# Sliding-window attention followed by a wave MLP: a reworked start, earlier and later loads, and a new order around the stage changes

## The chip, the cores and the metric

The kernel runs on one core of a Trainium2 chip. The metric is device time in microseconds (us) of one execution. Executions of one kernel on one chip mostly lie within 1 us of each other, and an effect of half a per cent is 0.9 us, so every claim below about time rests on a ratio of means with its 95% interval, and profiles (each is one execution) are used for where the time goes. An execution more than 1.5% above the fastest of its kernel is called slow and left out of the ratios.

## The reference

Four batches, eight heads, 768 positions, head size 64. Attention keeps the last 96 positions and 8 global ones, with a bias that falls linearly with distance. Its output x goes through a "wave" layer:

```
theta = x @ w_theta                       # 512 x 512
u     = x + w_tok_r @ (x*cos(theta)) + w_tok_i @ (x*sin(theta))    # tokens mixed, 768 x 768
out   = u + relu(u @ w_ch)                # 512 x 512
```

## The kernel before

The program first runs the attention of batch 0 in an order written by hand, then weaves the wave layer of batch b (dense work for TensorE) with the attention of batch b+1. Five engines take part: PE (TensorE), DVE (VectorE), ACT (ScalarE), POOL (GpSimd, which issues all loads that turn f32 into bf16, on one software queue, q0) and SP (SyncE, which issues output writes and the DMA transposes of x, u and of q and k of batch 3). An engine executes its instructions in program order. Where one instruction waits, all behind it on that engine wait too.

Loads of batch 3 come in "token" form, 128 tokens on the partitions, so that a DMA transpose can turn q and k without reordering copies. Each row is 64 numbers of f32, 256 bytes:

```python
def load_qk_tokens(b, h0, n):
    qk = loads[b][0]
    for h in range(h0, h0 + n):
        for i_ in range(2):
            pair = qk[:, i_, h // 2 * 2:h // 2 * 2 + 2].rearrange("p h t d -> p (h t d)")
            nc.gpsimd.dma_start(
                out=pair.rearrange("p (t h d) -> p t h d", t=NT, h=2)[:, :, h % 2],
                in_=(q, k)[i_][b, h].rearrange("(t p) d -> p t d", p=T))
```

Half of q and k of batch 3 is loaded while batch 0 is in its wave layer, the rest and v behind a gate, a GpSimd copy of one element of the transposed x of batch 1:

```python
def load_behind(b, tile):
    g = nc.gpsimd.tensor_copy(out=gate, in_=tile).ins
    with tc.issue_after(g):
        load_qk_tokens(b, H // 2, H // 2)
        load_all_v(b)
```

`kglob` builds kG from kT: k of each block with the 8 global positions copied over its front. In batch 3 these copies stand on VectorE among the products `zri` = x*cos, x*sin:

```python
def kglob(b, p):
    kT = qkT[(b, p)][1]
    kG = qkT[(b, p)][2] = att.tile([T, NT - 2, T], BF, name="kG", bufs=6)
    with behind("dve") if b == B - 1 else nullcontext():
        nc.vector.tensor_copy(out=kG, in_=kT[:, T:(NT - 1) * T].rearrange(...))
        nc.vector.tensor_copy(out=kG[:, :, 0:NG], in_=kT[:, None, 0:NG].to_broadcast(...))
```

The start of a batch: `th` are the six parts of theta, `rest` what is left of the channel step of the batch before.

```python
order = th[:4] + rest[:2] + th[4:] + rest[2:] if b else []
if b == 2:
    order[:0] = [lambda p=p: prep_dma(3, p) for p in range(1, NP)]   # DMA transposes of q, k
if b == 1:
    order.insert(0, lambda: load_behind(3, xT_sb[1][0:1, NC - 1, 0:1]))
```

The loop over head pairs in the attention of batch 0, cut. Each turn ends with the scores of the next pair and the transposes of the one after it:

```python
for p in range(NP):
    score_exp(0, p, 1)
    ...                                  # out0: kT on ACT, qT on DVE; kglob
    values(0, p - 1, 0); values(0, p - 1, 1)
    score_bias(p, 2); score_mms(0, p, 2); score_exp(0, p, 2)
    cast0(p + 2, 1, dve); cast0(p + 2, 0, dve)       # reordering copies
    ...
    score_bias(p + 1, 0); score_mms(0, p + 1, 0); score_exp(0, p + 1, 0)
    score_bias(p + 1, 1); score_mms(0, p + 1, 1)
    turn0(p + 2, 1); turn0(p + 2, 0)                 # 12 transposes
    ...
```

The softmax here doesn't subtract the row's maximum and nothing guards it: scores larger than these inputs give would overflow.

## Time and profile before

| | before |
|---|---|
| median of 3 executions | 175.34 us (175.04 to 175.66) |
| span of the profiled execution | 172.6 us |
| PE / DVE / ACT / POOL busy | 93 / 74 / 57 / 22% |
| first cosine of batches 0, 1, 2, 3 starts at | 29.91, 74.19, 108.03, 141.99 us |
| last u of batch 1 to first u of batch 2 | 105.60 to 117.72: 12.1 us |

The cosines are good milestones: each opens the wave layer of a batch, since ScalarE can start one only when x of that batch is complete, transposed and multiplied by `w_theta`. The lines of the profile that show what bounds the kernel are in the prediction below.

### The profile page before, as it was taken

To read this page: it belongs to the slowest core of one execution; us is meant where nothing else is said; L and a number is where in the kernel's file an instruction comes from. 1 tells how busy PE (TensorE), PEld (TensorE's weight loads), DVE (VectorE), ACT (ScalarE), POOL (GpSimd) and SP (SyncE) were. 2 spreads that over 40 slices of the span, in tenths; PEclk is the share of its full clock that TensorE was granted. 3 is DMA by queue.
4 is the path that set the end of the run, shared out by engine and by line. 5 is a ranking of instruction groups with operands and counts; after the bars stand their busy time and mean duration, and the time that the engine had idled before them with its cause. 6 is when DMAs were issued, how large, how long until landed. Compare 5 with 4: busy or idle time off the path is not lost.

```text
span 172.6 us, 3652 instructions
## 1 busy us (share of the span) xinstructions
PE 159.9 (93%) x1482; PEld 83.5 (48%) x1482; DVE 128.5 (74%) x288; ACT 99.1 (57%) x124; POOL 37.9 (22%) x45
## 2 busy tenths in 40 slices
PE   6479979999999999999999998999999989999991
PEld 1245655455756566544455463444554634444440
DVE  7678965678999999999587588597786837724443
ACT  2479676999497595489834740979348308500010
POOL 8974355005272010099300000000000000000000
PEclk9999999999999999999999999999999999999998
DMA  5999999999999999879999997787138571323335
GB/s 146 192 193 178 210 208 209 204 204 171 160 204 175 166 155 128 132 97 154 210 141 80 224 158 165 138 152 226 30 76 113 135 171 40 142 41 102 100 93 182
DMA packets 75088, 25.92 MB, mean 150 GB/s; under 512 B 63168, under 2 KB 72128, under 8 KB 75072
## 3 DMA queue, kind: packets, MB, share of 16 engines
q0 software_dynamic: 45680, 12.45, 78.4%
q1 hardware_dynamic: 28976, 12.72, 36.6%
q10 hardware_dynamic: 416, 0.52, 0.9%
q8 instruction: 11, 0.18, 0.4%
q14 instruction: 5, 0.04, 0.1%
HBM read 25.69 MB, written 6.29 MB: 185 GB/s over the span
## 4 chain that ended last, share of the span: by engine, by line
PE 59%; DVE 21%; ACT 10%; DMA 6%; issue 1%; SPq 0%; DVEq 0%; ACTq 0%
PE ps L409 29%; PE ps L434 10%; PE pb L389 5%; PE pb L295 4%; PE pb L352 4%; DVE x_sb L362 4%; ACT etab L142 3%; PE ps L389 3%; ACT e L302 3%; DMA qk<-in_k_dram 3%; DVE kG L218 2%; DVE e L312 2%; ACT cs L395 2%; DMA kT<-qk 2%; DMA xT<-x_sb 2%; PE ps L244 2%
## 5 line engine op out<-in xcount | busy, mean ns | idle before, releaser
L409 PE MATMUL ps<-zri,w_tokT 128*128 128x512 bf16 x288 | 70.6, 380 | 0.3 <-DVE o_sb L440 0.2
L302 ACT ACTIVATE e<-pb 128x1024 bf16<-128x1024 f32 (+1 forms) x48 | 43.6, 958 | 23.1 <-PE pb L295 22.9
L409 PEld LDWEIGHTS <-w_tokT 128*128 128x128 bf16 x288 | 26.1, 98 | 29.0 <-issue 1.0
L414 DVE TENSOR_TENSOR u<-x_sb,ps 128x512 bf16<-128x512 bf16 x24 | 16.4, 682 | 14.6 <-PE ps L409 14.6
L434 PE MATMUL ps<-w_ch_bf,uT 128*128 128x512 bf16 x96 | 24.2, 379 | 0.0
L398 DVE TENSOR_TENSOR zri<-x_sb,cs 128x512 bf16<-128x512 bf16 x48 | 17.9, 418 | 8.0 <-ACT cs L395 7.8
L440 DVE SCALAR_TENSOR_TENSOR o_sb<-ps,u 128x512 f32<-128x512 f32 (+1 forms) x25 | 16.5, 662 | 3.1 <-PE ps L434 3.1
L395 ACT ACTIVATE cs<-pb,halfpi 128x1024 bf16<-128x1024 f32 x8 | 8.9, 1116 | 15.7 <-PE pb L389 15.7
L312 DVE TENSOR_TENSOR e<-e,etab 128x1024 bf16<-128x1024 bf16 (+1 forms) x24 | 14.7, 615 | 3.4 <-ACT e L302 3.4
L389 PE MATMUL pb<-w_theta_bf,xT 128*128 128x512 bf16 x64 | 15.2, 379 | 1.0 <-DMA xT<-x_sb 1.0
L295 PE MATMUL pb<-qT,kT 64*128 64x128 bf16 x224 | 15.6, 219 | 0.6 <-DVE qT L211 0.3
L295 PEld LDWEIGHTS <-kT 64*128 64x128 bf16 x224 | 9.0, 94 | 14.1 <-issue 12.5
L389 PEld LDWEIGHTS <-xT 128*128 128x128 bf16 x96 | 9.0, 98 | 12.0 <-DMA xT<-x_sb 2.4
L428 ACT COPY uT<-ps 128x512 bf16<-128x512 bf16 x7 | 4.1, 587 | 18.6 <-PE ps L427 18.6
L352 PEld LDWEIGHTS <-e 128*128 128x128 bf16 x352 | 12.7, 97 | 3.3 <-issue 1.5
L434 PEld LDWEIGHTS <-uT 128*128 128x128 bf16 x96 | 8.9, 98 | 10.0 <-ACT uT L428 0.3
L295 PE MATMUL pb<-qT,kG 64*128 64x128 bf16 x128 | 11.7, 217 | 1.2 <-DVE kG L220 1.2
L88 POOL DMA_DIRECT2D vn<-in_v_dram x5 | 9.7, 1930 | 12.2 <-DVE vn L68 10.6
L362 DVE TENSOR_TENSOR x_sb<-pb,rec 128x768 bf16<-128x768 f32 x12 | 11.4, 949 | 0.3
L315 DVE TENSOR_TENSOR e<-e,etab 128x1024 bf16<-128x1024 bf16 x12 | 8.2, 684 | 2.8 <-ACT e L302 2.8
L352 PE MATMUL pb<-vn,e 128*128 128x65 bf16 x168 | 9.6, 193 | 0.3 <-DVE x_sb L362 0.3
L82 POOL DMA_DIRECT2D qk<-in_q_dram x8 | 7.4, 920 | 8.8 <-DVE qkn L229 5.0
(74 smaller groups left out, 203.0 us busy)
## 6 DMA issues: line engine op xcount, KB each, us to landing
out_dram<-o_sb SPq DMA_DIRECT2D x23, 256.0 KB, 2.4
vn<-in_v_dram POOLq DMA_DIRECT2D x3, 768.0 KB, 22.7
qk<-in_q_dram POOLq DMA_DIRECT2D x2, 768.0 KB, 21.0
qk<-in_k_dram POOLq DMA_DIRECT2D x2, 768.0 KB, 23.6
w_nat<-in_moe_w_tok_r_dram POOLq DMA_DIRECT2D x3, 384.0 KB, 13.7
w_nat<-in_moe_w_tok_i_dram POOLq DMA_DIRECT2D x3, 384.0 KB, 14.6
vn<-in_v_dram POOLq DMA_DIRECT2D x2, 384.0 KB, 8.9
qk<-in_q_dram POOLq DMA_DIRECT2D x8, 96.0 KB, 9.7
```

What stands on the lines that cost most here:

```text
L295: nc.tensor.matmul(pb[:, hh, o:o + T], lhsT=lhsT, rhs=qT[R, (own, nxt)[part]], start=bool(b), stop=bool(b) or (jt == NT - 1 or (j == 1 and ...
L302: ins = nc.scalar.activation(e_c, pb[:, :, 0:n], AF.Exp, scale=scale).ins
L312: nc.vector.tensor_mul(e_c, e_c, tab[:, :, s0:s0 + n // T].rearrange("p a s n -> p a (s n)"))
L352: nc.tensor.matmul(o, lhsT=l_, rhs=r_, start=(i_ == 0), stop=(i_ == len(mms) - 1))
L362: nc.vector.tensor_mul(xv, po4[:, :, :, 0:D], rec.to_broadcast([T, n, NT, D]))
L389: nc.tensor.matmul(pb[j_] if last else pb[:, j_, :], lhsT=xT[:, dc, st(j_)], rhs=w_theta_bf[:, dc, :], start=(dc == 0), stop=(dc == NC - 1))
L395: nc.scalar.activation(o, p_, AF.Sin, **bias)
L398: nc.vector.tensor_mul(zri[b][:, i_, 2 * c + j_, :].rearrange("p (g d) -> p g d", g=NP), xb[:, :, 2 * c + j_, :], cs[:, i_, j_].rearrange( ...
L409: anchor["pe"] = nc.tensor.matmul(ps, lhsT=w_tokT[wi][:, st, tt * T:(tt + 1) * T], rhs=zri[b][:, wi, st, :], start=(st == 0 and wi == 0), ...
L414: anchor["dve"] = nc.vector.tensor_add(u_sb[b, tt].rearrange("p (g d) -> p g d", g=NP), x_sb[b][:, :, tt, :], ps.rearrange("p (g d) -> p g ...
L434: nc.tensor.matmul(ps_c, lhsT=uT[:, dc, :], rhs=w_ch_bf[:, dc, :], start=(dc == 0), stop=(dc == NC - 1))
L440: nc.vector.scalar_tensor_tensor(o_sb[:, cols], in0=ps_c[:, cols], scalar=0.0, in1=u[:, cols], op0=ALU.max, op1=ALU.add)
```

## The change

The intent was to shorten the start (the first 42 us, where no engine is full), to free VectorE and GpSimd where VectorE is full (42 to 61 us), and to fill waits at the stage changes. Its parts, with names used from here on:

- **Front**: the reordering copies of batch 0 go, each head is transposed by itself into half of the columns; the order of the loop changes; the end of batch 0 is cut into pieces of tokens (4 blocks, then 2); kG of the first pair moves to ScalarE; one exponent table is built early; two of the loads of batch 0 change places.
- **qk1**: q and k of batch 1 are loaded ahead of the last token weights.
- **Loads of batch 3**: all of q and k of batch 3 now stand behind the gate.
- **Order**: one channel tile runs ahead of theta at the start of batches 1 to 3.
- **Tail**: the last channel tile is computed in two halves.

```diff
@@ front: half transposes
-            nc.tensor.transpose(ps[:, t_, :], qkn[:, t_, i_].rearrange("p h d -> p (h d)"), ident)
+    def turn(ps, src):
+        for t_ in range(NT):
+            for hh in range(2):
+                nc.tensor.transpose(ps[hh * D:(hh + 1) * D, t_, :], src[:, hh, t_, :], ident)
@@ front: loop, cut
+        score_bias(p + 1, 0)
+        score_mms(0, p + 1, 0)
         if p + 2 < NP:
-            cast0(p + 2, 1, dve)
-            cast0(p + 2, 0, dve)
+            turn0(p + 2, 1)
+            turn0(p + 2, 0)
+        score_exp(0, p + 1, 0)
+        score_bias(p + 1, 1)
+        score_mms(0, p + 1, 1)
@@ front: token pieces, cut
-    values(0, NP - 1, 0)
-    values(0, NP - 1, 1)
-    trans_w(0, nc.scalar.copy)
-    xtrans(0, NP - 1)
-    for c in range(NT // 2):
-        theta(0, c, 0)
-        theta(0, c, 1)
+    values(0, p, 0, 0, 4)
+    values(0, p, 1, 0, 4)
+    trans_w(0, act)
+    theta(0, 0, 2)
+    xtrans(0, p, dve, 0, 4)
+    values(0, p, 0, 4, 6)
+    values(0, p, 1, 4, 6)
+    theta(0, 1, 2)
+    xtrans(0, p, dve, 4, 6)
+    theta(0, 0, 3)
+    theta(0, 1, 3)
@@ qk1
+            if tt == NT - 4:
+                load_all_qk(1)
...
     load_w()
-    load_all_qk(1)
@@ loads of batch 3
-            load_qk_tokens(b, H // 2, H // 2)
+            alloc_qk(b)
+            load_qk_tokens(b, 0, H)
...
-            side.append((0, lambda: (alloc_qk(3), load_qk_tokens(3, 0, H // 2))))
@@ order
-        order = th[:4] + rest[:2] + th[4:] + rest[2:] if b else []
+        order = rest[:1] + th[:4] + rest[1:2] + th[4:] + rest[2:] if b else []
@@ tail: cut
+        parts = 2 if (b, tt) == (B - 1, NT - 1) else 1
+        n = DM // parts
+        pss_c = [ps_small([T, n], FP) for _ in range(parts)]
```

## The prediction

> **What bounds the kernel now.** I read the page's busy shares first, then the slices, then a table of stages (busy time per stretch), then the chain of waits in order of time, and last the DMA landings and the timeline around the places where the chain leaves TensorE.
>
> ```profile
> PE 159.9 (93%) x1482; PEld 83.5 (48%) x1482; DVE 128.5 (74%) x288; ACT 99.1 (57%) x124; POOL 37.9 (22%) x45
> PE   6479979999999999999999998999999989999991
> DVE  7678965678999999999587588597786837724443
> ACT  2479676999497595489834740979348308500010
> ```
>
> TensorE is the bound on average, but the three rows of tenths (4.3 us each) show that it is not the bound everywhere. In the first seven slices, the attention of batch 0, no engine is full; in slices 11 to 16 VectorE stands at 9 in every slice. So I cut the span at the places where the chain changes engine:
>
> ```profile
> 5.70:28.15 22.45, 18.66 (x285) 11.85 (x286) 18.19 (x49) 17.03 (x22) 14.21 (x17) 1.00 1.49 194
> 28.15:36.00 7.85, 7.81 (x45) 3.84 (x44) 4.79 (x12) 6.30 (x9) 0.26 (x1) 1.00 1.25 205
> 42.40:61.00 18.60, 17.80 (x233) 10.82 (x230) 18.54 (x42) 12.88 (x18) 5.74 (x7) 1.00 2.38 175
> 61.00:105.60 44.60, 44.33 (x438) 23.96 (x439) 37.27 (x79) 28.19 (x35) 10.56 (x11) 1.00 1.46 146
> ```
>
> Columns: stretch, its length, busy time and count of PE, PEld, DVE, ACT, POOL. A busy PE is pipelined, so I count its work by the distance between starts instead: a 512-column matmul costs 0.216 us (sixteen in 3.45 us on the chain), a 128-column transpose 0.056, a pair of score matmuls 0.056, a value matmul 0.03. By counts per stretch, 5.7 to 28.15 us holds about 14.6 us of such work in 22.4 (8 us slack), 28 to 42.4 is full, 42.4 to 61 holds 14.4 in 18.6 (4 us slack, VectorE 18.54 busy), and 61 to the end is nearly full. **What can be won lies before 61 us**, plus small holes later. The chain around the second stretch:
>
> ```profile
> 33.16 2.84 ACT cs L395 x5
> 36.01 1.28 ACT L142
> 37.31 5.12 ACT etab L142 x8
> 42.43 0.47 ACT uT L428
> 42.90 0.70 ACT kT L251
> 43.62 0.29 DVE kG L218
> ```
>
> After the sines of batch 0, ScalarE reloads its table and builds eight exponent tables; only then does it copy k of batch 1, and from there VectorE carries the chain to 61 us. A second thing gates the same point: k of batch 1 is issued at 21.85 us and takes 19.4 to land, so at 41.25, and VectorE's first reordering copy of batch 1 starts at that moment.
>
> ```profile
> 41.28 1.16 DVE L229 COPY qkn<-qk 128x768 bf16<-128x768 bf16 x4
> qk<-in_k_dram POOLq DMA_DIRECT2D x1, 768.0 KB, 19.4
> ```
>
> (From the timeline of VectorE and from the DMA issues of a window that holds that one issue.)
>
> **What the Trainium skill says.** (1) "TensorEngine Tiling (Array Packing)", Tiling Modes: tiles of the array run matmuls in parallel, and changing the mode drains it. Here six score matmuls in two row tiles take 0.34 us where six full transposes take 0.50 to 0.52, so row tiles do overlap; column tiles, which the new half-wide transposes use, do not occur in this trace. (2) "SBUF — State Buffer", Who interferes with whom: VectorE copies in a two-port mode and GpSimd lock each other out, and GpSimd writes the descriptors of its DMAs. The trace agrees: the kG copy (SBUF to SBUF) has a median of 0.290 us but 1.081 at 7.70 us, when POOL is issuing loads without a gap. (3) "ScalarE: Activation LUTs", What ACT_TABLE_LOAD costs: 1283 ns; the trace has three of 1283 ns.
>
> **The change, part by part.**
>
> *Reordering copies of batch 0.* Six VectorE copies (409 ns mean, 2.2 us) go. Instead each pair of heads is transposed one head at a time: 96 transposes for 48. If the two column halves overlap this costs TensorE nothing; if not, 48 x 0.056 = 2.7 us, in a stretch with 8 us slack. The kG copy of the first pair (1.08 + 0.17 us) moves to ScalarE in two parts, only the first of which (an estimate of 0.5 us with its small copy) stands ahead of the first scores. I expect the first exponential 0.3 to 0.6 us earlier than 9.32, mostly spent again because the second score chunk now waits behind both transposes of pair 1. The loop over pairs took 3.64, 3.72 and 4.94 us (ends of the second exponential: 11.26, 14.90, 18.62, 23.56). Its smallest cycle is exponential 0.97, kT copy 0.70, kG 0.62, scores 0.25, exponential 0.97 = 3.5 us. VectorE sat at about 5.0 us a turn in the slow turns and falls to 4 or less. So three turns of some 3.55 in place of 12.3: 1.6 us, and the last exponential, which started 0.93 us late behind the values and the transposes of x, comes right behind its predecessor: together **about 2.7 us** (end 25.3 to 22.6).
>
> *Token pieces at the end of batch 0.* Values, transposes of x and the first three quarters of theta are interleaved, so that TensorE's waits for VectorE (0.77 and 0.29 us at 22 to 25 us) are filled and theta starts near 24.5 instead of 28. Laying out the new order with the durations above I get theta complete near 30.4 instead of 33.2 us. But the first cosine needs theta(0,0,3), which now comes after both pieces: 28.3 against 29.9, a gain of only 1.5 us for ScalarE, whose 6.1 us of sines then run to 34.5. One table (0.64 us) has moved into ScalarE's idle time before the first load lands at 5.14, so the tables end at 34.5 + 1.3 + 7/8 x 5.1 = 40.2 instead of 42.4: **2.2 us of the 2.7 survive**.
>
> *q and k of batch 1 ahead of the last token weights.* The queue delivers in order at about 206 GB/s as written (each 384 KB matrix pair 1.8 us, a 768 KB load 3.9). Passing two token loads and the channel weights, k of batch 1 lands at 41.25 - 2 x 1.8 - 2.5 = 35 us. The last token weights slip from 31.0 to 38.8 us and the channel weights to 41.25; in this trace they are first used near 45 and at 49.9, so even 4 us earlier they are in time. VectorE can then do four of the reordering copies (1.16 us) in its idle time before 40 us: **another 0.5 to 1 us** for the stretch that VectorE bounds.
>
> *Loads of batch 3 behind x of batch 1.* Eight issues of 0.83 us (6.6 us of POOL) leave 46 to 63 us, where VectorE is full and its kG copies go from 0.29 to 0.57 us; I put 0.5 us on that, and 0.3 on transposing DMAs of x that took 8.7 and 5.0 us there against a median of 2.9. They move behind 70 us, sixteen issues in a row (13 us), with v of batch 3 landing near 100 us; its first use is after 105.
>
> *Later.* One leftover channel tile (four matmuls, 0.86 us) now runs before theta of batches 1 to 3 and covers the waits for the transposed x, 0.53 and 0.47 us: **about 0.8 us**. The last channel tile is computed in two halves, so VectorE starts its first half 0.4 us earlier: **0.3 us**.
>
> Sum: 2.2 + 0.7 + 0.6 + 0.8 + 0.3 = 4.6 us. One limit cuts it: v of batch 1 still lands at 48.0 us (the same bytes are ahead of it), and VectorE needs it at 50.8 now, so a shift of over 2.8 us before that point meets the load. I take off 0.2: **4.4 us, 170.9 us**.
>
> **The rivals.** (a) *The loads take over.* GpSimd's queue is full until about 60 us; k of batch 2 lands at 55.2 and v of batch 1 at 48.0, whatever the order in front. If they bind, the shift of the front is capped at about 2 us and the end is 172.5 to 173. For: the DMA row at 9 in slices 2 to 14. Against: only v of batch 1 sits within 3 us of its use. (b) *Column tiles do not overlap, or their mode changes drain TensorE*: 2.7 us more work in the startup, turns 0 and 1 above 4 us; gain in front about 1 us, end near 172.5. (c) *ScalarE keeps the second stretch*: sines and tables are a serial 12 us after the first cosine; if that starts as late as before, only the batch 3 and later parts remain, 173.5. (d) *More than I count*: VectorE, TensorE and loads all relieved at once between 36 and 61 us, where TensorE has 4 us slack; the shift at 61 could be 5 to 6, end 168.5. (e) *Sixteen token loads at 71 to 85 us* disturb the transposing DMAs of batch 2; TensorE is full there with work in hand, so under 0.5 us.
>
> **Range and chances.** Rivals a to c each take 1 to 2.5 us off and d adds as much: 168.4 to 173.3. The 2% mark is 171.8, 0.9 us above my number, so faster 0.68, within 2% 0.29. Nothing adds work on the dense part behind 61 us, so slower by 2% gets 0.03.
>
> **What would show it.** Last exponential of batch 0 ending at 22 to 23 us; first cosine near 28.3; last table near 40.2; k of batch 1 landing near 35 us; the chain leaving VectorE for TensorE near 57.5 instead of 61; no wait of theta for the transposed x at batches 2 and 3; 24 half transposes in about 0.7 us (overlap) or 1.4 (none). The prediction is wrong if the first cosine doesn't move, or if the dense part behind 61 us changes its length by over 1.5 us, since I assumed that it only shifts.

## The result and the profile after

After the change the median is 177.16 us (176.5 to 177.56, four executions) against 175.19 in the same rounds. A ratio compares the mean times of fast runs of the same rounds, so it is not quite the ratio of those medians: 1.0111, with a 95% interval of 1.0066 to 1.0156. The kernel became about 1% slower. A repeat on another chip gave 1.0101. All outputs are right. The predicted 170.9 and the whole range, 168.4 to 173.3, are missed.

The page of the kernel after: the total and the rows of engines in 40 slices, now 4.4 us each.

```profile
span 175.5 us, 3752 instructions
PE 160.7 (92%) x1534; PEld 83.9 (48%) x1534; DVE 125.7 (72%) x286; ACT 99.3 (57%) x127; POOL 38.0 (22%) x45
PE   7489789899999999999999996889999999999991
DVE  5737676678999999997768786088877865724442
ACT  4698583999497694389933810669545508500010
POOL 8965346005000000299940000000000000000000
```

Two things stand out. VectorE is less busy by 2.8 us, as intended. But PE shows a dip to 6 in slice 25 (105 to 110 us), where the row of before has an 8, and VectorE has a 0 in slice 26. The POOL row shows what moved: the loads of batch 3 now fill slices 17 to 21; before, half of those of q and k lay in slices 11 to 15.

The table of stages of the kernel after (stretch, length, busy time and count of PE, PEld, DVE, ACT and POOL, granted clock, DMA, GB/s), with a row for the change of batch 1 to 2 (the stretch in which batch 1 has ended and batch 2 not yet begun) that the prediction had not cut out:

```profile
5.70:28.15 22.45, 18.34 (x321) 11.60 (x322) 15.41 (x43) 17.49 (x25) 13.43 (x16) 1.00 1.50 191
42.40:61.00 18.60, 18.20 (x243) 11.36 (x242) 18.60 (x43) 13.01 (x18) 0.00 (x0) 1.00 2.31 174
61.00:105.60 44.60, 44.22 (x437) 23.75 (x437) 37.61 (x78) 27.96 (x35) 16.27 (x18) 1.00 1.42 135
105.60:122.00 16.40, 13.19 (x76) 5.45 (x74) 9.63 (x25) 9.49 (x12) 0.00 (x0) 1.00 0.80 160
```

And that same row of the kernel before:

```profile
105.60:122.00 16.40, 15.64 (x116) 6.93 (x115) 12.20 (x30) 12.55 (x15) 0.00 (x0) 1.00 0.72 165
```

From 105.6 to 122 us PE does 76 instructions where it did 116. In milestones, from the two profiles:

| us | before | after | difference |
|---|---|---|---|
| last exponential of batch 0 ends | 25.30 | 25.41 | +0.1 |
| first cosine, batch 0 | 29.91 | 30.62 | +0.7 |
| last exponent table ends | 42.43 | 42.51 | +0.1 |
| a group of three reordering copies on VectorE starts | 60.73 | 60.76 | 0.0 |
| last u of batch 1 starts | 105.60 | 105.98 | +0.4 |
| first u of batch 2 starts | 117.72 | 120.75 | +3.0 |
| first u of batch 3 starts | 150.62 | 153.28 | +2.7 |
| last channel matmuls start | 167.14 | 169.81 | +2.7 |

A single profile is good for some tenths of a us here, not more: in the second profile of the kernel after ("after again" below) the last exponential ends at 24.56, the first cosine comes at 29.74 and the group of copies at 59.89 us, so 0.9 us earlier, while the change of batch 1 to 2 is long there too (105.12 to 119.35 us).

So two questions need an answer. Why did the front, forecast to gain 2.2 us, bring 0.8 at most by 61 us? And what opened the hole of 2.7 us (14.8 in place of 12.1) between batches 1 and 2?

For the hole, here are the waits in 100 to 122 us (engine and line, what it waited for, us in all, times, longest), first before:

```profile
ACT cs L395 <- PE pb L389: 6.8, 1, 6.8
DVE kG L218 <- DMA kT<-qk: 0.7, 1, 0.7
PE pb L389 <- DMA xT<-x_sb: 0.5, 1, 0.5
```

then after:

```profile
ACT cs L406 <- PE pb L400: 9.6, 1, 9.6
DVE kG L222 <- DMA kT<-qk: 5.8, 1, 5.8
PE pb L400 <- DMA xT<-x_sb: 2.2, 2, 1.6
```

ScalarE waits for theta (`pb`), and theta waits for the transposed x. Independently of that, VectorE stands 5.8 us at a kG copy of batch 3 that waits for a transposed k, and the products that need the cosines stand behind it in program order. The chain of waits of the kernel after passes through exactly that:

```profile
110.99 3.59 DMA kT<-qk
114.60 0.29 DVE kG L222
```

Both are DMA transposes. So the next view is the DMA traffic of 88 to 100 us: packets, MB and share of the queue q0, and of issues their count and the median us from issue to landing. Before:

```profile
q0 software_dynamic: 3128, 0.40, 53.6%
uT<-u SPq DMA_TRANSPOSE x3, 3.5
xT<-x_sb SPq DMA_TRANSPOSE x2, 4.1
```

After:

```profile
q0 software_dynamic: 8163, 1.04, 192.6%
uT<-u SPq DMA_TRANSPOSE x2, 8.7
xT<-x_sb SPq DMA_TRANSPOSE x2, 9.1
```

Here the loads of batch 3 run on while the x of batch 2 is being turned, and a transpose takes 9 us in place of 4. That is a theory until the loads alone are moved.

### The profile page after: what moved, and what is told of

It reads as the page before. It is cut to its first block, busy times and chain, and to the rows that moved or that the text cites. A ratio compares the mean times of both kernels' runs of the same rounds, so it can differ in the third digit from the quotient of the medians.

```text
span 175.5 us, 3752 instructions
## 1 busy us (share of the span) xinstructions
PE 160.7 (92%) x1534; PEld 83.9 (48%) x1534; DVE 125.7 (72%) x286; ACT 99.3 (57%) x127; POOL 38.0 (22%) x45
## 2 busy tenths in 40 slices
DMA packets 75089, 25.94 MB, mean 148 GB/s; under 512 B 63168, under 2 KB 72128, under 8 KB 75072
## 4 chain that ended last, share of the span: by engine, by line
PE 56%; DVE 17%; ACT 10%; DMA 9%; POOL 3%; issue 2%; SPq 1%; DVEq 0%; ACTq 0%; POOLq 0%
PE ps L420 27%; PE ps L448 9%; DMA vn<-in_v_dram 7%; ACT cs L406 6%; PE pb L400 6%; PE pb L357 4%; PE pb L298 3%; POOL qk L73 2%; ACT e L308 2%; DMA kT<-qk 2%; DVE qT L252 2%; PE ps L400 2%; DVE e L317 2%; DVE x_sb L368 2%; PE ps L248 2%
## 5 line engine op out<-in xcount | busy, mean ns | idle before, releaser
L448 PE MATMUL ps<-w_ch_bf,uT 128*128 128x512 bf16 (+1 forms) x100 | 24.7, 371 | 0.0
L357 PEld LDWEIGHTS <-e 128*128 128x128 bf16 x352 | 12.7, 97 | 3.9 <-issue 1.7
L222 DVE COPY kG<-kT 128x512 bf16<-128x512 bf16 x15 | 4.2, 282 | 8.0 <-DMA kT<-qk 5.8
```

What stands on the lines that cost most here:

```text
L357: nc.tensor.matmul(o, lhsT=l_, rhs=r_, start=(i_ == 0), stop=(i_ == len(mms) - 1))
L448: nc.tensor.matmul(ps_c, lhsT=uT[:, dc, :], rhs=w_ch_bf[:, dc, i_ * n:(i_ + 1) * n], start=(dc == 0), stop=(dc == NC - 1))
```

## The experiments

The theories put to test were these. **L**: the late loads of batch 3 make the DMA transposes of batch 2 slow and cause the whole loss. **F**: the front costs time by itself. **O**: the new order costs time. Kernels named a_ are the kernel after with one part undone, b_ the kernel before with one part done, f_ variants of the front alone, c_ and d_ combinations. The kernel before ran beside each in the same rounds; its medians were 174.73, 174.59, 175.09, 174.77 and 174.75 us in the five groups.

| run | ratio to before | 95% interval | median us |
|---|---|---|---|
| a_b3early | 0.9997 | 0.9966 to 1.0028 | 174.88 |
| b_b3late | 1.0209 | 1.0154 to 1.0264 | 179.79 (half of the runs slow) |
| a_oldorder | 1.0256 | 1.0211 to 1.0302 | 179.36 |
| a_turns | 1.0128 | 1.0092 to 1.0165 | 176.87 |
| b_tail | 1.0009 | 0.9983 to 1.0035 | 174.86 |
| b_order | 0.9941 | 0.9921 to 0.9962 | 173.62 |
| c0 | 0.9969 | 0.9945 to 0.9993 | 173.97 |
| c1 | 0.9930 | 0.9908 to 0.9951 | 173.46 |
| b_qk1 | 0.9967 | 0.9928 to 1.0005 | 174.68 |
| b_front | 1.0054 | 1.0012 to 1.0097 | 176.17 |
| a_gate1 | 1.0085 | 1.0038 to 1.0133 | 177.00 |
| c2 | 0.9844 | 0.9803 to 0.9884 | 172.51 |
| after again | 1.0101 | 1.0058 to 1.0143 | 176.54 |
| f_nopieces | 1.0069 | 1.0036 to 1.0101 | 176.22 |
| f_warm | 1.0102 | 1.0057 to 1.0146 | 176.50 |
| c3 | 0.9893 | 0.9857 to 0.9930 | 173.01 |
| d0 | 0.9927 | 0.9911 to 0.9943 | 173.50 |
| c2 again | 0.9868 | 0.9850 to 0.9886 | 172.44 |

### The loads of batch 3: a_b3early, b_b3late, a_gate1

The kernel after, with the loads of batch 3 split as before:

```diff
-            alloc_qk(b)
-            load_qk_tokens(b, 0, H)
+            load_qk_tokens(b, H // 2, H // 2)
...
-            pass
+            side.append((0, lambda: (alloc_qk(3), load_qk_tokens(3, 0, H // 2))))
```

> The changed kernel with the loads of batch 3 put back as before (first half of q and k early, second half and v behind x of batch 1). Theory (loads): with everything behind x of batch 1, the software queue stays busy to about 102 us instead of 92, and the transposing DMAs of x and u of batch 2 take 7.7 to 10.5 us instead of 2.7 to 5.6; theta of batch 2 starts 2.7 us late. Undone: about 2 us faster than the changed kernel (2.75 back at 121 us, up to 0.7 lost again to slower VectorE copies at 42 to 61 us), so 174.5 to 175.5 us, ratio to before 0.995 to 1.002. Rival (the leftover channel tile put ahead of theta makes the hole): stays at 176.5 to 177.5.

Measured: 0.9997. The loss is gone, and so is the hole's growth: last u of batch 1 to first u of batch 2 takes 12.0 us. The DMA traffic of 88 to 100 us is light again and the transposes are short:

```profile
q0 software_dynamic: 1523, 0.19, 27.6%
uT<-u SPq DMA_TRANSPOSE x3, 2.9
xT<-x_sb SPq DMA_TRANSPOSE x2, 2.8
```

What follows is that this one part costs 1.1% of the kernel, all of its loss. All other parts together are then worth nothing, where the forecast had 3.8 us for them.

The mirror image is the kernel before with all loads of batch 3 behind the gate (the same edit in reverse).

> The kernel before with one part alone: all loads of batch 3 behind x of batch 1. Theory (loads): 1.5 to 3 us slower than before, 176.7 to 178, with waits of theta of batch 2 for the transposed x of 1.5 us or more, and kG copies of 0.28 us at 42 to 61 us. Rival (channel tile order): same as before or up to 0.7 us faster.

Measured: 1.0209 from the three runs that count as fast; three more were slower still and left out. (The clock has a share in this number; see "Is it the clock?".) The queue is as busy as in the kernel after (7,965 packets in 88 to 100 us), its transposes of x take 8.8 us, and without the new order theta finds nothing to do in their place. The timeline of PE of this run (start, duration, what, and in brackets the idle time before it and its releaser):

```profile
108.84 1.81 PE L389 MATMUL pb<-w_theta_bf,xT 128*128 128x512 bf16 x4 [3.47 <-DMA xT<-x_sb]
```

The change of batch takes 16.7 us in place of 12.1. The cause works alone, then.

If the loads make the transposes slow, moving the loads earlier in batch 1 must move the damage. a_gate1 is the kernel after with the gate on an earlier part of x of batch 1:

```diff
-            order.insert(0, lambda: load_behind(3, xT_sb[1][0:1, NC - 1, 0:1]))
+            order.insert(0, lambda: load_behind(3, xT_sb[1][0:1, 1, 0:1]))
```

> The changed kernel with the same loads of batch 3 in the same order, but let go by the second block of x of batch 1 instead of the last, some 10 us earlier. Theory (256-byte packets of the software queue hold up the transposing DMAs of batch 2 while they last): the queue is done before 94 us, the transposing DMAs of x of batch 2 land in under 6 us, and 1.5 to 2.5 us come back: 174.5 to 175.5. Rival (it is the sixteen loads in one block, or the missing early half, that costs, not when they end): stays above 176.5.

Measured: 1.0085, no better than the kernel after within the intervals. The time is the rival's (above 176.5 us), not the theory's. The trace shows why. In 88 to 100 us the transposes are short again:

```profile
uT<-u SPq DMA_TRANSPOSE x3, 2.8
xT<-x_sb SPq DMA_TRANSPOSE x2, 2.7
```

but now those of batch 1, in 66 to 72 us, are the slow ones (2.8 us in the kernel after in that window):

```profile
q0 software_dynamic: 4163, 0.52, 172.0%
xT<-x_sb SPq DMA_TRANSPOSE x2, 6.9
```

The change of batch 1 to 2 is back to 12.0 us, while the first cosine of batch 1 comes at 77.75 us in place of 75.20. Whichever transposes the loads meet pay for it. So the rival does not explain the hole, which is gone although the sixteen loads still come in one block; and the forecast of theory L failed because it overlooked the transposes of batch 1. In the traces the cost followed the loads.

The Trainium skill, "DMA: Bandwidth & Descriptors", Issuing engines are not separate DMA queues, says that DMAs issued by any engine run on the same 16 DMA engines and interleave. The traces agree: with the packets of q0 adding up to 193% of the time that 16 engines have, against 28% in a_b3early, the transposes that SP issues take three times as long. The loads are made of 256-byte rows (of 75,089 packets in the profile of the kernel after, 63,168 are under 512 bytes), which are many packets for few bytes: 1.04 MB in 8,163 packets, so some 128 bytes each as written in bf16.

### The new order: a_oldorder, b_order

The kernel after with the old order:

```diff
-        order = rest[:1] + th[:4] + rest[1:2] + th[4:] + rest[2:] if b else []
+        order = th[:4] + rest[:2] + th[4:] + rest[2:] if b else []
```

> The changed kernel with the leftover channel tiles back behind the first two thirds of theta. Theory (loads): within 0.6 us of the changed kernel (176.6 to 177.6), the hole at theta of batch 2 stays. Rival (order makes the hole): 174.5 to 175.5.

Measured: 1.0256. Theta of batch 2 then waits 2.11 and 1.46 us for the transposed x where it waited 0.62 and 1.63. Theory O falls: the order hides up to 1.4% of the time in this kernel, more than it gains alone, because the wait that it covers has become larger. The expectation under theory L, within 0.6 us of the kernel after, missed this. Part of the 1.4% is a half-speed stretch of the clock behind the longer hole (below).

The order alone on the kernel before:

> The kernel before with one part alone: one leftover channel tile ahead of theta in batches 1 to 3. Prediction's step: 0.8 us faster (the two waits of theta for the transposed x, 0.53 and 0.47 us, are filled). Theory now: theta of batch 1 is pushed back by 0.4 us, as in the changed kernel, and batches 2 and 3 gain 0.5 each at most: 0.3 to 0.7 us faster. Rival: nothing or slower, since the first cosine waits longer for theta.

Measured: 0.9941, 1.0 us. No theta of batches 1 to 3 waits for a DMA any more; at batch 2 its sixteen matmuls run without a gap behind the channel tile:

```profile
105.55 1.03 PE L434 MATMUL ps<-w_ch_bf,uT 128*128 128x512 bf16 x4
106.41 3.62 PE L389 MATMUL pb<-w_theta_bf,xT 128*128 128x512 bf16 x16
```

The forecast of the prediction for this part, 0.8 us, held; the more cautious 0.3 to 0.7 of the expectation was too low.

### The tail: b_tail

The kernel before with the last channel tile in two halves.

> The kernel before with one part alone: the last channel tile computed in two halves. In all three kernels with the halves so far, the end came 5.6 to 6.2 us after the first of the last channel matmuls, in the two without them 5.46 us: VectorE finishes 0.27 us earlier, but the last writes land in 2.0 to 2.9 us instead of 1.8. Theory (the writes crowd): 0.1 to 0.7 us slower than before. Rival (the prediction's step): 0.3 us faster.

Measured: 1.0009 (0.9983 to 1.0035), nothing. The last two writes of the kernel before are issued by SP and ACT and land after 1.8 us each. The last of them (KB, us to landing):

```profile
out_dram<-o_sb ACTq DMA_DIRECT2D x1, 128.0 KB, 1.8
```

In b_tail:

```profile
out_dram<-o_sb ACTq DMA_DIRECT2D x1, 128.0 KB, 2.1
```

VectorE ends 0.27 us earlier, but the last write takes 0.3 us longer.

### The front: a_turns, b_front, f_nopieces, c0, c1

b_front is the kernel before with the front part alone (its diff is the one shown above under front).

> The kernel before with the front parts alone: half-wide transposes, reordered scores and copies of batch 0, and the token pieces at its end; loads, channel tile order and tail as before. Prediction's step: 2.2 us faster. Theory now (the transposes between the score chunks cost ScalarE 0.63 us a turn, which eats what the dropped copies gave; the pieces let TensorE finish theta earlier but start the sines no earlier): within 0.5 us of before, first cosine 29.5 to 30.6 us. From the ratios so far (changed kernel with loads put back 0.9997, order alone 0.9941, tail alone 1.0009) the front should even cost 0.5%, 0.8 us.

Measured: 1.0054 (1.0012 to 1.0097). The part that was to gain 2.2 us loses 0.9. Here is why it does not gain. The timeline of ScalarE of the kernel after, in the loop over pairs:

```profile
12.31 1.02 ACT L308 ACTIVATE e<-pb 128x1024 bf16<-128x1024 f32 x1
13.96 1.02 ACT L308 ACTIVATE e<-pb 128x1024 bf16<-128x1024 f32 x1 [0.63 <-PE pb L298]
```

and what PE does between the first and second chunk of scores of that turn:

```profile
12.19 0.86 PE L202 MATMUL ps<-ident,qk 128*64 128x128 bf16 x24
12.99 0.60 PE L278 MATMUL pb<-dist,diag 128*128 128x512 bf16 x2
13.53 0.23 PE L298 MATMUL pb<-qT,kT 64*128 64x128 bf16 x2
```

Twenty-four half transposes and the bias matmuls of the next chunk are done in order, 1.3 us, while ScalarE needs 1.02 for its exponential. So it waits 0.63 us for the second chunk, in the next turn 0.64. In the third turn it waits 1.46 us, there for the first chunk. The ends of the second exponentials lie at 10.75, 14.98, 19.22 and 24.03 us: turns of 4.23, 4.24 and 4.81 us, where the forecast had 3.55 and the kernel before 3.64, 3.82 and 4.84. The first exponential did start 0.72 us earlier (8.60 against 9.32), and in this profile the loop used that up. In the third turn VectorE waits for a load, v of heads 4 to 7:

```profile
18.83 0.43 DVE L338 COPY vG<-vn 128x1040 bf16<-128x1040 bf16 x1 [1.23 <-DMA vn<-in_v_dram]
```

That wait belongs to this execution and not to the kernel. In the profile of after again, which is the same kernel, VectorE does not wait there, and the third turn begins after 0.23 us:

```profile
21.21 1.94 ACT L308 ACTIVATE e<-pb 128x1024 bf16<-128x1024 f32 x2 [0.23 <-PE pb L298]
```

Its turns take 4.23, 4.23 and 3.58 us. The wait between the chunks of scores is in both profiles. Profiles with the same front differ by this much: the first cosine comes at 29.74 to 30.62 us in six with the new front and its token pieces, and at 29.61 to 29.97 in six with the old front. So the front did not bring it forward beyond that spread, where 1.5 us were forecast.

a_turns moves the half transposes behind the second chunk's scores, and the copy of v shown above (L338) one turn later:

```diff
-        if p + 2 < NP:
-            turn0(p + 2, 1)
-            turn0(p + 2, 0)
         score_exp(0, p + 1, 0)
         score_bias(p + 1, 1)
         score_mms(0, p + 1, 1)
+        if p + 2 < NP:
+            turn0(p + 2, 1)
+            turn0(p + 2, 0)
```

> The changed kernel with the half-wide transposes of a later pair behind the second score chunk (where they were before), and the second half of the global v copies one turn later. Theory (startup): in the changed kernel these transposes stand between the two score chunks of a pair and make ScalarE wait 0.63 us in each of two turns, and v heads 4 to 7 landing at 18.8 us hold VectorE for 1.2 us; without both, the last exponential of batch 0 ends near 23 to 23.7 us instead of 25.4, and the first cosine starts near 28.7 instead of 30.6. If a shift in front travels to the end, as the prediction assumed, the total is 1.5 to 2 us under the changed kernel (175.2 to 175.7). Rival (the front is absorbed by VectorE, loads or the batch 3 loads): total within 0.5 us of the changed kernel although the first cosine moves.

Measured: the turns take 3.48, 3.90 and 4.32 us, the wait in the first turn is gone (0.55, 0.81 and 1.55 us stay in the later ones), and the first cosine comes at 29.65 us (28.7 was expected). That is 0.97 earlier than in the first profile of the kernel after, but only 0.09 earlier than in the second, where the last exponential even ends before that of a_turns (24.56 and 24.80 us): what the first two turns win, the third loses. The time agrees: 1.0128, not distinguishable from the kernel after. The mechanism of the wait is shown by the trace; a gain in time from its repair, in this kernel, is not.

Is it the token pieces? f_nopieces is b_front with the end of batch 0 as before:

```diff
-    values(0, p, 0, 0, 4)
-    values(0, p, 1, 0, 4)
+    values(0, p, 0)
+    values(0, p, 1)
     trans_w(0, act)
-    theta(0, 0, 2)
-    ...
+    xtrans(0, p, dve)
+    for c in range(NT // 2):
+        theta(0, c, 0)
+        theta(0, c, 1)
```

> The front parts alone, without the token pieces (values, transposes of x and theta of the end of batch 0 in the order of before). Theory (the pieces let TensorE end theta earlier but start ScalarE's sines later, 5.2 us behind the last exponential instead of 4.6): first cosine 0.5 to 0.7 us earlier than in b_front relative to the last exponential, total 0.3 to 0.7 us under b_front (ratio 1.0054), so 0.999 to 1.004. Rival (the half-speed window of TensorE's clock at the start makes b_front slow, pieces or not): 1.004 to 1.007.

Measured: 1.0069, as b_front. The number is that of the rival, but its cause is not there: the profile has no half-speed window. The theory's gain is in the trace and does not reach the end. The first cosine comes at 29.10 us, 0.8 earlier than in the kernel before, and the second u of batch 0 at 39.86 in place of 40.67. Then the shift meets a load that is still where it was. The timeline of VectorE of f_nopieces:

```profile
39.86 0.69 DVE L423 TENSOR_TENSOR u<-x_sb,ps 128x512 bf16<-128x512 bf16 x1 [0.40 <-PE ps L418]
...
41.58 0.90 DVE L231 COPY qkn<-qk 128x768 bf16<-128x768 bf16 x3 [0.76 <-DMA qk<-in_k_dram]
```

It waits 0.76 us for k of batch 1, and the shift is gone. So a shorter front needs qk1 as its companion. The token pieces themselves cost here: from the end of the last exponential to the first cosine it takes 4.7 us without them (24.38 to 29.10) and 5.2 with them in both profiles of the kernel after (25.41 to 30.62, 24.56 to 29.74), since theta(0, 0, 3), the quarter that the first cosine needs, stands behind theta(0, 1, 2) and the transposes of the second piece.

c0 and c1 test that on top of the repairs so far. c0 is the kernel after with the loads of batch 3 and the tail as before and the loop of a_turns:

> The changed kernel with the loads of batch 3 put back, the half-wide transposes behind the second score chunk with the second half of the global v copies a turn later, and the last channel tile whole again. If a shift in front travels to the end and the causes add up: 174.9 (loads put back) minus 1.0 (the first cosine at 29.65 instead of 30.62 us) minus 0.3 (tail) = 173.6 us, ratio to before 0.992 to 0.996. If the front is absorbed by the loads or by VectorE: 174.5 or more.

c1 is c0 with that quarter of theta moved up:

```diff
+    theta(0, 0, 3)
     theta(0, 1, 2)
     xtrans(0, p, dve, 4, 6)
-    theta(0, 0, 3)
     theta(0, 1, 3)
```

> As c0, and the last quarter of theta of the first token piece ahead of the second piece's theta, so that ScalarE's serial sines start earlier. Theory (ScalarE's sines and tables carry 30 to 42 us): the first cosine 0.9 to 1.2 us earlier than in c0, and the total 0.7 to 1.1 us under c0, near 172.7. Rival (TensorE or VectorE carries this stretch): the first cosine moves but the end does not, within 0.3 us of c0.

Measured: c0 0.9969, just above the range of its first forecast, and c1 0.9930. In c1 the first cosine follows the last exponential after 3.9 us (24.99 to 28.88). The two ran in the same rounds, medians 0.5 us apart and intervals that still overlap at their edges, so the step from c0 to c1 is likely but not shown by itself. (In the profile of c0 the first cosine comes at 30.57 us, 0.9 later than in a_turns with the same front; a half-speed window of the clock lies in it, next section but one.)

### q and k of batch 1 earlier: b_qk1

> The kernel before with one part alone: q and k of batch 1 ahead of the last token weights. Prediction's step: k of batch 1 lands near 35 instead of 41.3 us and VectorE's reordering copies start earlier, 0.5 to 1 us faster. Theory now (the copies wait for their place in VectorE's order, behind the second u of batch 0, and the landing at 41.25 was a coincidence): k lands near 36 us, the first of these copies still starts right after that u, total within 0.3 us of before.

Measured: 0.9967 (0.9928 to 1.0005), so perhaps 0.6 us, perhaps nothing. The load itself came as forecast: issued at 14.30 us, it takes 20.8 us and lands at 35.1. But VectorE does not start the reordering copies earlier:

```profile
40.44 0.69 DVE L416 TENSOR_TENSOR u<-x_sb,ps 128x512 bf16<-128x512 bf16 x1 [0.40 <-PE ps L411]
41.04 1.16 DVE L231 COPY qkn<-qk 128x768 bf16<-128x768 bf16 x4
```

They stand behind the second u in VectorE's program, and start when it ends. In the kernel before they also started right behind the second u (40.67, copies at 41.28). That the load landed at 41.25 in that trace was a coincidence; it did not hold them.

### Is it the clock? f_warm, c3

The granted clock is the share of its full speed at which TensorE is allowed to run, as the profiler records it. Some profiles show it at half for 3.4 us around 8 to 12 us. In the profile of b_front the clock row has a dip, and 24 half transposes took 1.49 us in place of 0.86:

```profile
PEclk9979999999999999999999999999999999999999
8.70 1.49 PE L200 MATMUL ps<-ident,qk 128*64 128x128 bf16 x24
```

The Trainium skill, "TensorE: Matmul & The Clock Gate", HAM oscillation, gives idle gaps of PE of over about 3.4 us as what halves the clock. In b_b3late the trace agrees: behind theta's gap of 3.47 us the clock is at half from 109.0 to 112.4 us. In b_front it does not: the longest idle gap that the profile shows ahead of the dip is 1.29 us. The page's next section, "A second HAM failure mode: psum-queue depth-cycling", tells of a kernel whose frequent short idle times made the clock swing, which fits better.

The traces show a sum at work and not one long gap. In their clock records, full clock lasts 3.41 us or a whole multiple of it. Cut into pieces of 3.41 us, the 20 traces hold 939 pieces at full clock before the last matmul. In eight of them PE was busy for 1.59 us or less, and the clock was at half in the next piece; in the other 931 it was busy for 1.64 us or more, and the clock stayed. Here are two pieces of b_front and then two of the kernel before, a near miss (columns as in the table of stages):

```profile
4.46:7.87 3.41, 1.52 (x27) 0.89 (x26) 2.33 (x6) 2.19 (x7) 3.41 (x4) 1.00 1.25 186
7.88:11.29 3.41, 3.13 (x42) 2.07 (x41) 1.87 (x6) 2.14 (x4) 3.41 (x5) 0.50 2.07 168
3.86:7.27 3.41, 1.64 (x17) 0.98 (x16) 1.94 (x7) 1.82 (x4) 3.41 (x6) 1.00 1.37 235
7.28:10.69 3.41, 2.04 (x31) 1.36 (x30) 3.00 (x9) 1.37 (x2) 2.83 (x3) 1.00 1.99 172
```

Where the pieces begin differs from execution to execution: in the profiles with the new front the first full grant comes between 4.0 and 7.1 us, and the window followed in those where it came at 4.3 to 4.9. The ends of matmuls in a trace are modelled, and this is read from traces; no kernel was built to test it.

f_warm fills PE's idle time in the front of b_front with nine matmuls of zeros, and c3 does the same to c2:

```diff
+    warm(4)
     turn0(0, 1)
...
+    warm(5)
     kglob(0, 0, 0, 1, act)
```

> b_front with nine matmuls of zeros put where TensorE waits at the start (four ahead of the first transposes, five ahead of the first scores). In five of nine profiles of kernels with the new front the granted clock fell to half for 3.4 us near 8 to 12 us, in none of five with the old front. Theory (TensorE's idle time there lets the clock fall): no such window, clock at 0.995 or more, total 0.2 to 0.9 us under b_front: ratio 1.000 to 1.004. Rival (the window has another cause, or costs nothing since ScalarE carries that stretch): ratio 1.004 to 1.007.

> As c2 (ratio 0.9844), with the same nine matmuls of zeros. Theory (clock): 0.2 to 0.9 us under c2, ratio 0.979 to 0.984, no half-speed window at the start. Rival: 0.983 to 0.988.

Measured: f_warm 1.0102, c3 0.9893, where b_front has 1.0054 and c2 0.9844 and 0.9868; both lie above all that was expected. As a repair it fails. As a test of the clock it says more, since each execution's mean clock is recorded, profiled or not: a window of 3.4 us at half clock in 174 us makes a mean of 0.990. Below 0.9935 lie 0 of 55 executions of the kernel before, 0 of 24 of kernels with the old front (b_tail, b_order, b_qk1, d0), 23 of 63 with the new front (the six of a_oldorder aside, which has a second window later), and 0 of 12 with the new front filled. So the fill does remove the window: in f_warm and c3, PE is busy for 3.3 us of the first full piece. The count says nothing about old against new front, though, since the clock record begins with the first full grant and reads 1.00 before it. The six matmuls of zeros at the start take 0.43 us each in every trace, where later ones of 512 columns take 0.216:

```profile
1.19 2.74 PE L175 MATMUL ps<-zero 128*128 128x512 bf16 x6 [1.19 <-DVE zero L105]
```

In four of the six profiles with the old front (b_order, b_tail, d0, b_b3late) the first grant comes as late as 9.4 to 11.5 us, and 12 transposes take 1.46 us there in place of 0.92. That half-speed stretch is in no mean clock. Within one kernel, executions with the window are longer by 0.5 us (standard error 0.12, all those kernels pooled, one slow run left out): 0.2 us in the mean. The zeros cost as much or more: c3 takes 173.1 us, and c2 without the window 172.3 (mean over seven executions). The window is real and small, and it does not explain b_front: its four executions with it average 176.28 us, its two without 176.16.

The long hole in batch 2 brings a window of its own, in b_b3late as said and in a_oldorder from 110.6 to 114.0 us. Of six executions of b_b3late the one without any window took 177.24 us, the one with one 178.82, and four below 0.984 had a mean of 180.2. Three of the four are slow and left out; the fourth is in the ratio, and the executions of a_oldorder lie at 0.978 to 0.990. So 1.0209 and 1.0256 hold the damage of the loads together with the half clock that follows from it. The execution of b_b3late with full clock is 2.4 us longer than the mean of the kernel before.

### What a version without the failed steps is worth: c2, d0, after again, c2 again

One wait is left in c1. The timeline of VectorE, at the change of batch 1 to 2:

```profile
110.35 0.29 DVE L222 COPY kG<-kT 128x512 bf16<-128x512 bf16 x1 [3.07 <-DMA kT<-qk]
110.55 0.75 DVE L409 TENSOR_TENSOR zri<-x_sb,cs 128x512 bf16<-128x512 bf16 x2
```

A kG copy of batch 3 that nobody needs yet waits for its transposed k, and holds the products behind it. GpSimd has nothing to do then, so c2 gives it these copies:

```diff
         kG = qkT[(b, p)][2][:, t0:t1]
+        if b == B - 1:
+            copy = nc.gpsimd.tensor_copy
```

> As c1, with the kG copies of batch 3 on GpSimd instead of VectorE. In c1 VectorE waits 3.07 us for the transposed k of batch 3 in front of the products of batch 2 that TensorE needs, which took back 0.8 us of the 1.26 us gained in front. Theory: that wait goes, mix of batch 2 starts right behind theta, 0.5 to 1 us under c1 (173.5), near 172.7. Rival (ScalarE's sines bind there): the same as c1 within 0.3 us.

Measured: 0.9844 (0.9803 to 0.9884); the repeat beside d0 gave 0.9868 (0.9850 to 0.9886). The change of batch takes 11.0 us. The copies by tile, in the repeat (duration ns minimum, median, maximum, then first and last start):

```profile
L224 DVE COPY kG<-kT x11: 271/281/537, 12.5 to 72.5; 128x512 bf16<-128x512 bf16 x11
L224 POOL COPY kG<-kT x4: 703/781/974, 100.1 to 117.1; 128x512 bf16<-128x512 bf16 x4
```

A copy takes GpSimd 781 ns where VectorE needs 281, and it pays, because nothing else stands behind it there. c2 is faster than both kernels: 1.3 to 1.6% than before, and, over both ratios to before, about 2.5% than the kernel after.

> The best version again (0.9844 on another chip), beside d0. It differs from d0 by the mended new front, whose first cosine came at 28.9 to 29.6 us in three profiles against 29.9. Theory (with the loads early enough and the hole of batch 2 gone, a shift in front travels to the end): 0.3 to 1 us under d0. Rival (the new front is worth nothing even when mended): within 0.3 us of d0, or above it.

How much of that is the mended front? d0 is the kernel before with order, qk1 and the GpSimd copies, and the old front:

> The kernel before with three things: one channel tile ahead of theta (0.9941 alone), q and k of batch 1 ahead of the last token weights (0.9967 alone), and the kG copies of batch 3 on GpSimd; its old front stays. If the first two add up and the third takes away VectorE's wait for the transposed k: ratio 0.983 to 0.990.

Measured: 0.9927, against 0.9868 for c2 in the same rounds: medians 173.50 and 172.44, so the mended front is worth 1.06 us. It can gain, though not the 2.2 us of the forecast, and here it stands with theta's quarter moved, q and k of batch 1 loaded early and the wait in batch 2 gone; which of these it needs was not taken apart. The two profiles do not show the gain at its place: the first cosine comes at 29.61 us in d0 and at 29.70 in c2 again, whose profiled execution has the half-speed window; in c1, with the same front and without that window, it comes at 28.88. The ratio of d0 lies above the expected range. Order and qk1 alone multiply to 0.9908, so with the old front the copies on GpSimd add nothing that can be seen.

The repeat of the kernel after, on another chip:

> The changed kernel once more, unaltered, on the chip of the runs beside it, so that its size is known from six more executions: ratio to before 1.007 to 1.015.

Measured: 1.0101 (1.0058 to 1.0143), against 1.0111 at first. The result stands.

## Why the prediction was wrong

| step of the sum | forecast us | measured us |
|---|---|---|
| front (reordering, token pieces) | -2.2 | +0.9 alone (b_front) |
| q and k of batch 1 | -0.7 | -0.6 alone, the interval touches 0 |
| loads of batch 3 | -0.6 | +3.7 alone (b_b3late, with its clock; +2.4 at full clock), +2.0 within the change (1.0111 to 0.9997) |
| order | -0.8 | -1.0 alone |
| tail | -0.3 | +0.2 alone, nothing within its interval |

The measured column multiplies ratio minus one by 175 us. The entries do not add up to the result, because the parts act on each other: the order hides up to 2.5 us of the damage of the loads (1.0256 to 1.0111), and a front without qk1 runs into the load of k. The sum of the prediction also has a slip: its text puts 0.5 and 0.3 us on the loads, its sum 0.6.

**Failed: the loads of batch 3, rival (e).** The prediction saw the rival and wrote it off: "TensorE is full there with work in hand, so under 0.5 us". Three runs and their transposes show that it was the main effect. The flaw was to ask whether TensorE had work at 71 to 85 us, when the loads are issued. The queue ran on to about 102 us (94 before), into the change of batch 1 to 2, and there TensorE has no other work: theta needs the transposed x, at once. The trace of before even held the number: the prediction quotes transposes of 8.7 and 5.0 us beside the same loads at 42 to 61 us, against 2.9. It priced getting rid of that at 0.3 us and its return elsewhere at nothing. The gain on that side was true and small: in 42 to 61 us the kG copies take 0.28 us throughout, where one took 0.57 before, and POOL's busy time there is 0.00 for 5.74.

**Failed: the loop of the front.** The prediction put a turn at 3.55 us by a cycle through ScalarE and VectorE ("exponential 0.97, kT copy 0.70, kG 0.62, scores 0.25, exponential 0.97"). It left out TensorE, because its busy time had slack, although its order had changed: half transposes and bias matmuls now stood between two chunks of scores. Slack in a stretch says nothing about the order of work inside it. The first two turns became longer, 4.23 and 4.24 us where the kernel before has 3.64 and 3.82 (the prediction reads 3.72: it ends the second turn at 18.62 us, where the next instruction starts, and not at 18.72, where the exponential ends). The three turns take 13.3 us, and 12.0 in the second profile, against 12.3; 10.65 was forecast.

**Failed: the token pieces.** The prediction noted that the first cosine has to wait for theta(0, 0, 3) behind both pieces, and still took 1.5 us of gain from the shift of the last exponential, of which 2.7 us were forecast and none or 0.7 came (25.41 and 24.56 us against 25.30). Of themselves the pieces lengthen the way from the last exponential to the first cosine, 5.2 us in place of 4.6 in the kernel before. Theta as a whole is complete earlier (32.6 in place of 33.2 us), but nobody waits for its end.

**Half right: q and k of batch 1.** k lands at 35.9 us in the kernel after, 35 was forecast. That it "gates the same point" was read from two equal times, 41.25 and 41.28; the copies followed the second u in program order. The load matters only once the front is shorter (f_nopieces).

**Right on its part: the order.** 0.8 forecast, 1.0 us measured alone, and theta's waits at batches 2 and 3 are gone in b_order. In the kernel after theta waits at batch 2 again, for the reason above.

**Failed, but small: the tail.** VectorE's 0.3 us were counted as time; the last writes gave them back.

**Rival (b)** was wrong, as the prediction held: 24 half transposes take 0.86 us, so the column halves overlap. The sign that the prediction named for being wrong, a dense part behind 61 us that changes its length by over 1.5 us, was met: 61 us to the last channel matmuls is 2.6 us longer.

**Open.** b_front costs half a per cent by itself and no run isolates why. Its profile is level with that of the kernel before at the last u of batch 1 (105.53 and 105.60 us) and loses 0.8 us at the change of batch 1 to 2 (12.9 against 12.1). Theta waits no longer there than before (0.54 and 0.53 us), but VectorE's kG copy waits 1.48 us for the transposed k in place of 0.69, and the products of batch 2 stand behind it. Ahead of that, about 106 us, a transpose of u takes 4.2 to 4.4 us in profiles with the new front (a_b3early, b_front, f_nopieces, c0, c1, both of c2) and 2.5 in five with the old front, with no load left in q0; in f_warm and c3 it takes 2.6 and 2.5. Nothing tried here explains that. It would fit that c2, which takes that copy off VectorE, is where the front gains; this was not tested alone. And f_warm is as slow without the long transpose. A second loss, of 0.3 us, comes at batch 3, where theta's wait is 0.82 us in place of 0.47. The profile of b_tail also has 12.7 us at that change, with no loss in its mean time, so one profile is thin evidence. Whether 256-byte rows or the sheer number of bytes make the loads so harmful to transposes was not tested either.

## What to carry to other kernels

Before moving a load to a quiet time, look at where its queue will end, not where it is issued, and at which transfers with someone waiting on them run there; the busy share of the compute engines does not show it. Busy time with slack does not say that new work fits: on an engine that works in order, write down what stands between a result and the instruction that waits for it. Test the parts of a change one at a time: here one part cost 1%, the order part alone gained 0.6%, and the version that beat both kernels keeps most of the change, mends two of its waits, moves one group of copies to GpSimd, and leaves out that part and the tail.

## What the Trainium skill lacked or had wrong

- "DMA: Bandwidth & Descriptors", Issuing engines are not separate DMA queues: it says that all DMAs share 16 engines and interleave, but gives no measure of what a transpose suffers. Here a DMA transpose of x took 2.8 us beside a light software queue (1,523 packets in 12 us) and 9.1 beside a full one (8,163 packets, 1.04 MB, in 12 us), and the kernel lost 1.1% by it.
- "TensorE: Matmul & The Clock Gate", HAM oscillation: its limit for the halving of the clock is an idle gap of over about 3.4 us, and frequent short ones stand in the section after it as a second case, without a number. Here the half-clock window of 3.4 us came in 23 of 63 executions of the new front with gaps of at most 1.29 us seen in the profile of b_front; nine matmuls in the gaps removed it in 12 of 12. It cost 0.5 us when it came. In the traces, the clock fell after each of the eight 3.41 us pieces in which PE was busy for 1.59 us or less, and after none of 931 with 1.64 us or more. The page does speak of activity windows of this length, but does not say how busy PE has to be in one to keep the clock.
- "TensorEngine Tiling (Array Packing)", Tiling Modes: it says that a change of mode drains the array, without a price. Here, between row-tiled matmuls at 12.03 us and full ones at 12.99, 24 transposes in two column tiles take 0.80 us from start to start; at the 0.056 us of a full transpose for each pair of halves that would be 0.67. So by this estimate all losses together, drains included, are 0.13 us at most.
- No page that was consulted gives times of this copy on the two engines: 128 x 512 in bf16 takes GpSimd 781 ns (703 to 974; spans on GpSimd are rough in a profile) and VectorE 281.
